# Streamed attention weights in row blocks of 128 x 1536 instead of column blocks of 640 x 384, with five ring slots instead of three

## The chip, the cores and the metric

The kernel runs on one core of one Trainium2 chip. The metric is the device time of that core in microseconds (us), the median over several executions. The kernel before was measured again beside every experiment. Its median lay between 2383 and 2409 us from one batch of runs to another, so kernels of different batches are compared by their ratio to the kernel before of the same batch.

## The reference, cut to what matters

```python
# x: 2048 x 640, H = 32 heads, Dh = 192, M = 8 memory tokens, seg = 32 tokens, all bf16
mem = mem0
for s in range(64):
    xs = x[:, s*32:(s+1)*32, :]
    h  = concatenate([mem, xs], axis=1)            # 40 rows x 640
    q, k, v = h@Wq, h@Wk, h@Wv                     # 640 x 6144 each
    p  = softmax(masked(q@k^T * Dh**-0.5))         # per head, 40 x 40
    o  = (p@v) @ Wo                                # 6144 x 640
    mem = o[:, :8, :]                              # the next segment needs it
    outs.append(o[:, 8:, :])
a = concatenate(outs)
b = gelu(x@w_gate) * (x@w_up) @ w_down             # 640 -> 1536 -> 640
g = sigmoid(sum(x * gate_w))
out = g*a + (1-g)*b
```

The 64 segments form a chain: the memory rows that one segment returns are inputs of the next. Each segment multiplies only 40 rows with all four attention matrices (31.5 MB). The memory plan of each kernel has room for only a part of them (47 of 64 pieces before, 61 of 84 after). That part stays resident, and the rest is loaded again in every segment.

## The kernel before

The attention weights are cut into 64 pieces of 480 KB. A Q, K or V piece is 128 partitions x (5 row blocks x 384 columns), that is, all 640 rows of two heads. A Wo piece is three row blocks of 128 x 640. 47 pieces are resident. 17 are streamed in every segment through a ring of three slots, by DMAs that the SP engine issues. A streamed piece is first copied once to a contiguous scratch in HBM and read from there.

```python
B_RING = int(opts.get("ring", 3))
...
def piece_src(m, t):
    if m == 0:
        return Wq2[:, :, 384 * t:384 * t + 384]        # [p, k, n]: 5 row blocks x 384 columns
    ...
    return Wo2[:, 3 * t:3 * t + 3, :]
...
def piece(seg, m, t):
    ...
    while done <= pos:
        slot = stream_counter[0] % B_RING
        if not (seg == 0 and done < B_RING):
            S_.add("sp", lambda e, slot=slot, done=done: e.dma_start(ring_flat[slot], wscr[done]),
                   reads=[Rg("dw", done, done + 1)], writes=[r_ring[slot]],
                   dma_sem="ring%d" % slot, name="ring s%d p%d" % (seg, done))
```

A load into a slot waits until the matmuls that read the slot's last piece are done. The Q and K projections take one piece at a time, chunk by chunk, with the row blocks innermost. The score matmuls of a group of four heads use eight tiles of 128 rows and then eight of 64 rows, because a head has 192 columns:

```python
def qk_pair(s, pr):
    for ti in range(2):
        for m in range(2):
            pv_, pr_ = piece(s, m, t)
            for cc in range(3):
                for k in range(KT):                    # KT = 5, innermost
                    fns.append(... e.matmul(ps[:, bank, slot*R:(slot+1)*R], pv_[:, k, cc*128:(cc+1)*128],
                                   Hb[hb][:, k, :], start=(k == 0), stop=(k == KT - 1)))   # L826
...
def scores(s, o):
    ...
    fa.append(... Q[:, qs, :], Q[:, ks, :], tile_position=(0, 0) ...)
    fa.append(... Q[:, qs + 2, :], Q[:, ks + 2, :], tile_position=(0, 64) ...)
    fb.append(... Q[0:64, qs + 1, :], Q[0:64, ks + 1, :], tile_position=(0, 0) ...)
    fb.append(... Q[64:128, qs + 1, :], Q[64:128, ks + 1, :], tile_position=(64, 64) ...)
    S_.add("pe", fa + fb, ...)
```

The order of work in a segment ends with `("wo", 3), ("pt", 3), ("wo", 4), ("pv", 3), ("wo", 5), ("wo", 6), ("wo", 7)`: "pt" transposes the probabilities of the last heads, "pv" multiplies them with V, and each "wo" is 30 matmuls of the output projection.

Of the kernel before, what the change touches and what calls it, by code (L numbers as in the profile page):

```python
# [221 lines left out]
def _build(nc, A_x, A_mem0, A_Wq, A_Wk, A_Wv, A_Wo, seg_len, w_gate, w_up, w_down,  # L222
# [23 lines left out]
    PIECE = KT * 384 * 2  # L246
    assert 3 * Dm * 2 == PIECE
# [21 lines left out]
    wsA["Hx"] = al(2 * KT * 128 * 2)  # L269
# [7 lines left out]
    wsA["xr4"] = al(Dm * 2)  # L277
    NQB, NVB, NPB, NUB = 3, 2, 2, 2
    wsB["QKT"] = al(NQB * 12 * R * 2)
    wsB["v"] = al(NVB * 768)  # L280
    wsB["vl"] = al(NOCT * 768)
    wsB["p"] = al(NPB * 4 * 64 * 2)
# [3 lines left out]
    wsB["stats"] = al(2 * 3 * 4 * 4)  # L286
    wsB["aT4"] = al(KT * 128 * 2)
    wsB["br4"] = al(Dm * 2)
# [15 lines left out]
    npieces = 4 * NT  # L304
    B_RING = int(opts.get("ring", 3))
    nslots = (total - wsA_total - wsB_total) // PIECE
    nres = min(npieces, nslots - B_RING)
    if "nres" in opts:
        nres = min(nres, int(opts["nres"]))
    nstream = npieces - nres  # L310
    if nstream == 0:
        B_RING = 0
    assert nres >= 0 and nres + B_RING <= nslots and (nstream == 0 or 2 <= B_RING <= nstream)
    arena_bytes = max((nres + B_RING) * PIECE + wsB_total, B_RING * PIECE + ffn_total) + wsA_total
    arena_bytes = al(arena_bytes)
    assert arena_bytes <= total, (arena_bytes, total)
# [6 lines left out]
    assert ffn_base >= B_RING * PIECE  # L323
    ring_off = [j * PIECE for j in range(B_RING)]
    res_off = [(B_RING + j) * PIECE for j in range(nres)]
    o = wsA_base - wsB_total
    assert o >= (nres + B_RING) * PIECE
# [15 lines left out]
    slot_class = []  # L343
    for j in range(nres):
        end = res_off[j] + PIECE
        if end <= ffn_base:
            slot_class.append(0)
        elif end <= ffn_off["wd"]:
            slot_class.append(1)
        else:  # L350
            slot_class.append(2)
    late_slots = [j for j in range(nres) if slot_class[j] > 0]

# [14 lines left out]
    Hx = [bview(o_Hx + b * KT * 256, KT * 256).rearrange("p (k t) -> p k t", t=128) for b in range(2)]  # L368
    r_Hx = [sreg(o_Hx + b * KT * 256, KT * 256) for b in range(2)]
# [15 lines left out]
    xr4 = bview(wsA_off["xr4"], Dm * 2)  # L385
    r_xr4 = sreg(wsA_off["xr4"], Dm * 2)
    QB = 12 * R * 2
    QKT = [bview(wsB_off["QKT"] + b * QB, QB).rearrange("p (s r) -> p s r", r=R) for b in range(NQB)]
    r_QKT = [sreg(wsB_off["QKT"] + b * QB, QB) for b in range(NQB)]
# [4 lines left out]
    pm_sb = [bview(wsB_off["p"] + b * 512, 256).rearrange("p (t k) -> p t k", k=L) for b in range(NPB)]  # L394
    pl_sb = [bview(wsB_off["p"] + b * 512 + 256, 256).rearrange("p (t k) -> p t k", k=L) for b in range(NPB)]
    r_p = [sreg(wsB_off["p"] + b * 512, 512) for b in range(NPB)]
# [13 lines left out]
    br4 = bview(wsB_off["br4"], Dm * 2)  # L410
    r_br4 = sreg(wsB_off["br4"], Dm * 2)
    r_br4h = [sreg(wsB_off["br4"], Dm * 2, 0, 4 * XA), sreg(wsB_off["br4"], Dm * 2, 4 * XA, 128)]
    r_xr4h = [sreg(wsA_off["xr4"], Dm * 2, 0, 4 * XA), sreg(wsA_off["xr4"], Dm * 2, 4 * XA, 128)]
    mem0r = br4
    r_mem0r = r_br4
    gwr = bview(wsB_off["aT4"], 256)
    r_gwr = sreg(wsB_off["aT4"], 256)
    assert wsB_off["aT4"] >= ffn_off["brow"] and wsB_off["br4"] >= ffn_off["brow"]
# [28 lines left out]
    def piece_src(m, t):  # L447
        if m == 0:
            return Wq2[:, :, 384 * t:384 * t + 384]
        if m == 1:  # L450
            return Wk2[:, :, 384 * t:384 * t + 384]
        if m == 2:
            return Wv2[:, :, 384 * t:384 * t + 384]
        return Wo2[:, 3 * t:3 * t + 3, :]

    def piece_view(m, o):
        if m == 3:
            return bview(o, PIECE).rearrange("p (c n) -> p c n", n=Dm)
        return bview(o, PIECE).rearrange("p (k n) -> p k n", n=384)

    PROG = [("qk", 0), ("qk", 1), ("qk", 2), ("sc", 0), ("v", 0), ("qk", 3), ("qk", 4), ("pt", 0), ("sc", 1),
            ("v", 1), ("qk", 5), ("pv", 0), ("qk", 6), ("pt", 1), ("sc", 2), ("v", 2), ("qk", 7), ("pv", 1),
            ("wo", 0), ("wo", 1), ("pt", 2), ("sc", 3), ("v", 3), ("pv", 2), ("wo", 2), ("wo", 3), ("pt", 3),
            ("wo", 4), ("pv", 3), ("wo", 5), ("wo", 6), ("wo", 7)]
    assert NOCT == 4
    COST = dict(qk=0.4, v=1.0, sc=0.45, pt=0.1, pv=0.45, wo=0.4)
# [3 lines left out]
    for kind, i in PROG:  # L470
        if kind == "qk":
            for ti in range(2):
                for m in range(2):
                    order.append((m, 2 * i + ti))
                    tcons.append(tt)
                    tt += COST[kind]
        elif kind == "v":
            for tl in range(4):
                order.append((2, 4 * i + tl))
                tcons.append(tt)  # L480
            tt += COST[kind]
        elif kind == "wo":
            for ti in range(2):
                order.append((3, 2 * i + ti))
                tcons.append(tt)
                tt += COST[kind]
        else:
            tt += COST[kind]
    tseg = tt + 0.6
    assert len(order) == npieces and len(set(order)) == npieces  # L490
    streamed = set()
    for k in range(nstream):
        target = (k + 0.5) * tseg / nstream
        best = min((i for i in range(npieces) if i not in streamed), key=lambda i: abs(tcons[i] - target))
        streamed.add(best)
    resident_list = [i for i in range(npieces) if i not in streamed]
    stream_list = [i for i in range(npieces) if i in streamed]
    res_slot = {}
    for k, i in enumerate(resident_list):
        res_slot[order[i]] = k  # L500
    stream_pos = {order[i]: k for k, i in enumerate(stream_list)}
    r_res = [sreg(o, PIECE) for o in res_off]
    r_ring = [sreg(o, PIECE) for o in ring_off]
    if nstream > 0:
        wscr = nc.dram_tensor("w_stream_scratch", (nstream, 128, PIECE // 2), BF, kind="Internal").ap()
    ring_flat = [bview(o, PIECE) for o in ring_off]
# [3 lines left out]
    order_index = {mt: i for i, mt in enumerate(order)}  # L510
    last_req = {}

    def piece(seg, m, t):
        oi = order_index[(m, t)]
        assert oi == last_req.get(seg, -1) + 1, "pieces must be consumed in `order`"
        last_req[seg] = oi
        if (m, t) in res_slot:
            j = res_slot[(m, t)]
            return piece_view(m, res_off[j]), r_res[j]
        pos = stream_pos[(m, t)]  # L520
        done = issued.get(seg, 0)
        while done <= pos:
            mm, tq = order[stream_list[done]]
            slot = stream_counter[0] % B_RING
            if not (seg == 0 and done < B_RING):
                S_.add("sp", lambda e, slot=slot, done=done: e.dma_start(ring_flat[slot], wscr[done]),
                       reads=[Rg("dw", done, done + 1)], writes=[r_ring[slot]],
                       dma_sem="ring%d" % slot, name="ring s%d p%d" % (seg, done))
            stream_counter[0] += 1
            ring_of[(seg, mm, tq)] = slot  # L530
            done += 1
        issued[seg] = done
        slot = ring_of[(seg, m, t)]
        return piece_view(m, ring_off[slot]), r_ring[slot]

    def resident_load_ops(classes):
        ops = []
        for k, i in enumerate(resident_list):
            if slot_class[k] not in classes:
                continue  # L540
            m, t = order[i]

            def reg(k=k, m=m, t=t):
                dst = piece_view(m, res_off[k])
                src = piece_src(m, t)
                S_.add("sp", lambda e: e.dma_start(dst, src), writes=[r_res[k]], dma_sem="res%d" % k,
                       name="res %d %d" % (m, t))
            ops.append(reg)
        return ops

    def relayout_ops():
        nb = B_RING
        seq = list(range(nb, nstream)) + [(nstream - nb + j) % nb for j in range(nb)]
        loads = []
        stores = []
        for i, k in enumerate(seq):
            slot = i % nb
            assert k >= nb or k == slot
            m, t = order[stream_list[k]]

            def ld(k=k, slot=slot, m=m, t=t):
                S_.add("sp", lambda e: e.dma_start(piece_view(m, ring_off[slot]), piece_src(m, t)),
                       writes=[r_ring[slot]], dma_sem="ring%d" % slot, name="relay ld %d" % k)

            def st(k=k, slot=slot):
# [526 lines left out]
```

## Time and profile before

| quantity | before | where it is read |
|---|---|---|
| median time | 2409.07 us (4 runs, 2389.05 to 2410.3) | the runs |
| span of the profiled execution | 2396.1 us | the page |
| PE busy | 86% | the page |
| time of one segment | 34.31 us | mean distance of the memory copies on ACT |
| start of segment 0's memory copy | 230.4 us | the same |
| PE waits for streamed weights, from 232 us on | 120 us | the waits view, summed over lines |
| PE waits named "issue", from 232 us on | 144 us | the same |
| PE waits for other engines, from 232 us on | 22 us | the same |

These are lines of the page of the kernel before: the busy times, two of the DMA queues (packets, MB, share of the 16 DMA engines), the shares of the chain of waits that ended last, the costliest group (busy us, mean ns, then the idle time before it and what ended most of it), and one line of the DMA issues (KB each, us from issue to landing).

```profile
span 2396.1 us, 128172 instructions
PE 2064.1 (86%) x60326; PEld 1704.8 (71%) x60326; DVE 852.3 (36%) x2880; ACT 629.3 (26%) x1432; POOL 37.9 (2%) x181
...
q1 hardware_dynamic: 201578, 581.72, 76.4%
...
q8 instruction: 471, 7.72, 1.3%
...
PE 55%; DMA 38%; issue 6%; SPq 0%; ACT 0%; DVE 0%; DVEq 0%
...
L826 PE MATMUL ps<-arena 128*128 128x40 bf16 x30720 | 902.9, 182 | 190.3 <-issue 104.4
...
arena<-w_stream_scratch SPq DMA_DIRECT2D x1085, 480.0 KB, 4.5
```

PE (matmuls) and PEld (weight loads, which overlap them: 2064.1 and 1704.8 us busy in a span of 2396.1) are the busiest engines, and everything else is far from full. The chain is PE 55% and DMA 38%: by this line alone, the streamed weights seem worth a third of the time. The waits view shows how much PE stands. These are its largest lines for PE (line, waited for; us in total, times, longest us):

```profile
PE ps L826 <- issue: 104.4, 122, 2.5
...
PE ps L826 <- DMA arena<-w_stream_scratch: 57.8, 86, 2.1
...
PE ps L962 <- DMA arena<-w_stream_scratch: 33.9, 66, 2.5
...
PE ps L843 <- DMA arena<-w_stream_scratch: 24.6, 45, 2.0
```

L826 is the Q and K projections, L962 is Wo and L843 is V. Two kinds of stop matter: a weight piece that has not landed, and "issue", where PE waits for nothing that the profile names. Both kinds show in the timeline of PE (start, duration, group; the wait just before it in brackets):

```profile
1008.43 0.53 PE L962 MATMUL ps<-arena 128*128 128x40 bf16 x15
1009.49 2.25 PE L962 MATMUL ps<-arena 128*128 128x40 bf16 x75 [0.52 <-DMA arena<-w_stream_scratch]
...
1015.70 1.07 PE L826 MATMUL ps<-arena 128*128 128x40 bf16 x32
1018.22 0.88 PE L826 MATMUL ps<-arena 128*128 128x40 bf16 x28 [1.45 <-issue]
```

The "issue" stop of 1.45 us falls in the middle of one run of L826 matmuls. Such stops are those of instruction fetch. The queue line has 471 instruction transfers with 7.72 MB, 16 KB each, and PE runs 120,652 instructions (60,326 matmuls and as many weight loads), that is 471 blocks of 256. Counting PE's instructions in blocks of 256, in the records of the trace from about 200 us on, 159 of the 343 gaps over 0.5 us between weight loads stand at one of two neighbouring places of the block in the kernel before (the others include the waits for weights).

### The profile page before, as it was taken

The numbers are of one execution on the slowest core, as the hardware profiler recorded it, in microseconds if no ns is written. First come the engines' busy times: TensorE is split into PE (matmuls) and PEld (weight loads), VectorE is DVE, ScalarE is ACT, GpSimd is POOL, SyncE is SP. The second block draws the span as 40 slices with busy tenths as digits, with TensorE's granted clock in tenths as the row PEclk, the third lists the DMA queues.
The fourth block names the chain that finished last, engine by engine and source line by source line (L and its number), as shares of the span: only waits on it lengthen the run. The fifth ranks groups of instructions, "written<-read, shape, count | busy, mean of one in ns | idle before, by whom it ended". The sixth has DMA issues, their size and how long they took to land.

```text
span 2396.1 us, 128172 instructions
## 1 busy us (share of the span) xinstructions
PE 2064.1 (86%) x60326; PEld 1704.8 (71%) x60326; DVE 852.3 (36%) x2880; ACT 629.3 (26%) x1432; POOL 37.9 (2%) x181
## 2 busy tenths in 40 slices
PE   7997888888889888898888888888888888888887
PEld 3455777777777777777777777777777777777776
DVE  2222343333334333343334333333433333333333
ACT  2222222222222222222222222222222222222222
POOL 0000000000000000000000000000000000000000
PEclk9998999999999999999999999999999999999999
DMA  8868878787887887777787878777887777878777
GB/s 291 275 199 262 255 251 250 248 263 246 254 252 252 256 254 250 258 244 245 250 262 239 254 249 252 251 246 249 248 265 234 239 253 249 260 244 257 244 241 231
DMA packets 210940, 600.41 MB, mean 251 GB/s; under 512 B 19426, under 2 KB 68074, under 8 KB 210410
## 3 DMA queue, kind: packets, MB, share of 16 engines
q1 hardware_dynamic: 201578, 581.72, 76.4%
q10 hardware_dynamic: 8832, 10.49, 1.3%
q8 instruction: 471, 7.72, 1.3%
q14 instruction: 59, 0.48, 0.1%
HBM read 578.53 MB, written 13.60 MB: 247 GB/s over the span
## 4 chain that ended last, share of the span: by engine, by line
PE 55%; DMA 38%; issue 6%; SPq 0%; ACT 0%; DVE 0%; DVEq 0%
DMA arena<-w_stream_scratch 37%; PE ps L826 24%; PE ps L843 11%; PE ps L962 7%; PE ps L726 2%; PE ps L723 2%; PE ps L741 2%; PE ps L933 1%; PE ps L881 1%; PE ps L865 1%; DMA arena<-in_B_w_up_dram 1%; PE ps L877 1%; PE ps L935 0%; PE ps L744 0%; ACT arena L1002 0%
## 5 line engine op out<-in xcount | busy, mean ns | idle before, releaser
L826 PE MATMUL ps<-arena 128*128 128x40 bf16 x30720 | 902.9, 182 | 190.3 <-issue 104.4
L826 PEld LDWEIGHTS ps<-arena 128*128 128x128 bf16 x30720 | 845.0, 97 | 292.9 <-issue 182.6
L830 ACT ACTIVATE arena<-ps 128x480 bf16<-128x480 f32 x512 | 291.9, 570 | 867.2 <-PE ps L826 859.3
L962 PE MATMUL ps<-arena 128*128 128x40 bf16 x15360 | 446.8, 180 | 42.8 <-DMA arena<-w_stream_scratch 33.9
L962 PEld LDWEIGHTS ps<-arena 128*128 128x128 bf16 x15360 | 422.4, 96 | 64.4 <-DMA arena<-w_stream_scratch 45.3
L843 PE MATMUL ps<-arena 128*32 128x384 bf16 x6400 | 338.4, 348 | 35.4 <-DMA arena<-w_stream_scratch 24.6
L916 DVE TENSOR_TENSOR arena<-ps,arena 128x320 bf16<-128x320 bf16 x256 | 125.8, 491 | 397.2 <-PE ps L914 397.2
L843 PEld LDWEIGHTS ps<-arena 128*32 128x32 bf16 x6400 | 154.1, 100 | 125.2 <-DMA arena<-w_stream_scratch 30.9
L893 DVE TENSOR_REDUCE arena<-ps 104x4 f32<-104x160 f32 x256 | 81.3, 318 | 319.6 <-PE ps L883 319.2
L947 DVE CAST arena<-ps 64x160 bf16<-64x160 f32 x256 | 80.6, 315 | 261.4 <-PE ps L935 261.3
L897 ACT ACTIVATE ps<-ps 104x160 f32<-104x160 f32 x256 | 71.9, 281 | 350.4 <-DVE ps L895 350.4
L943 ACT ACTIVATE arena<-ps 128x320 bf16<-128x320 f32 x256 | 111.2, 434 | 183.0 <-PE ps L935 183.0
L850 ACT ACTIVATE arena<-ps 128x384 bf16<-128x384 f32 x256 | 124.8, 488 | 43.8 <-PE ps L843 42.6
L933 PE MATMUL ps<-arena 128*128 128x160 bf16 (+1 forms) x768 | 131.4, 259 | 4.6 <-issue 2.1
L935 PE MATMUL ps<-arena 128*128 128x64 bf16 (+1 forms) x768 | 126.0, 203 | 2.9 <-issue 2.8
L899 DVE TENSOR_REDUCE arena<-ps 104x4 f32<-104x160 f32 x256 | 83.1, 325 | 99.7 <-ACT ps L897 98.2
L933 PEld LDWEIGHTS ps<-arena 128*128 128x128 bf16 x768 | 73.6, 98 | 33.4 <-issue 12.3
L895 DVE TENSOR_TENSOR ps<-ps,arena 104x160 f32<-104x160 f32 x256 | 85.1, 332 | 8.8
L949 DVE CAST arena<-ps 64x160 bf16<-64x160 f32 x256 | 83.9, 328 | 7.9
L881 PE MATMUL ps<-arena 64*40 64x40 bf16 x1024 | 71.0, 182 | 12.4 <-DMA arena<-w_stream_scratch 8.0
L1004 DVE CAST arena<-ps 128x120 bf16<-128x120 f32 x64 | 18.1, 282 | 168.1 <-ACT arena L1002 166.3
L903 DVE TENSOR_TENSOR arena<-ps,arena 104x128 bf16<-104x128 f32 x256 | 74.6, 291 | 8.8
(73 smaller groups left out, 1473.6 us busy)
## 6 DMA issues: line engine op xcount, KB each, us to landing
arena<-w_stream_scratch SPq DMA_DIRECT2D x1085, 480.0 KB, 4.5
w_stream_scratch<-arena SPq DMA_DIRECT2D x17, 480.0 KB, 6.9
arena<-in_A_Wv_dram SPq DMA_DIRECT2D x16, 480.0 KB, 7.3
arena<-in_A_Wk_dram SPq DMA_DIRECT2D x16, 480.0 KB, 7.0
arena<-in_A_Wq_dram SPq DMA_DIRECT2D x16, 480.0 KB, 5.7
arena<-in_A_Wo_dram SPq DMA_DIRECT2D x16, 480.0 KB, 8.9
arena<-in_A_x_dram SPq DMA_DIRECT2D x4, 640.0 KB, 7.1
ffn_b_scratch<-arena ACTq DMA_DIRECT2D x16, 160.0 KB, 5.5
```

The costliest lines, as they stand in the source:

```text
L826: e.matmul(ps[:, bank, slot * R:(slot + 1) * R], pv_[:, k, cc * 128:(cc + 1) * 128], Hb[hb][:, k, :], start=(k == 0), stop=(k == KT - 1)))
L830: S_.add("act", lambda e: e.activation(out=QKT[b], in_=ps[:, bank, 0:12 * R].rearrange("p (s r) -> p s r", r=R), func=ACTF.Copy), reads=[r ...
L843: fns.append(lambda e, k=k, j=j: e.matmul(ps[32 * j:32 * j + 32, bank, 0:384], lhs(k), pvs[j][0][:, k, :], start=(k == 0), stop=(k == KT - ...
L850: S_.add("act", lambda e: e.activation(out=v_sb[o % NVB], in_=ps[:, bank, 0:384], func=ACTF.Copy), reads=[r_ps[bank]], writes=[r_v[o % NVB ...
L881: fb.append(lambda e, Q=Q, o0=o0, qs=qs, ks=ks: e.matmul(o0, Q[0:64, qs + 1, :], Q[0:64, ks + 1, :], start=False, stop=True, tile_position ...
L895: S_.add("dve", lambda e: e.tensor_tensor(out=S3, in0=S3, in1=mxb, op=ALU.subtract), reads=[rb, rst], writes=[rb], name="smax sub")
L916: S_.add("dve", lambda e: e.tensor_tensor(out=PTm, in0=apx(pv[:, 512:616], [[64, 2], [0, 4], [1, R]]), in1=apx(mbd, [[0, 2], [1, 4], [0, R]]),
L933: return [lambda e: e.matmul(full, v[:, e0:e0 + 128], PTm[:, ia:ib], start=True, stop=False, skip_group_check=True), lambda e: e.matmul(pa ...
L935: lambda e: e.matmul(part, vl[:, e0:e0 + 128], PTl[:, ia:ib], start=False, stop=True, skip_group_check=True)]
L943: S_.add("act", lambda e: e.activation(out=apx(u[:, 0, 0, :], [[2 * R, 2], [3 * R, 4], [1, R]]), in_=ps[:, A, 0:2 * W].rearrange("p (c t r ...
L949: S_.add("dve", lambda e: e.tensor_copy(out=u[64:128, :, 1, :], in_=ps[64:128, B, W:2 * W].rearrange("p (t r) -> p t r", r=R)), reads=[r_p ...
L962: fns.append(lambda e, pv_=pv_, cc=cc, c=c, n=n, t=t, u=u: e.matmul(ps[:, OB, n * R:(n + 1) * R], pv_[:, cc, n * 128:(n + 1) * 128], u[:, ...
```

## The change

The intent is to make the ring deeper for little more memory (5 x 384 = 1920 KB instead of 3 x 480 = 1440 KB) and to do without the scratch copy. The Q, K and V weights are cut into row blocks: 128 rows x 1536 columns (eight heads) of 384 KB, read from the inputs as they lie. Wo pieces shrink from three row blocks to two (320 KB). 61 of 84 pieces are resident, 23 are streamed per segment (16 and 7), and the ring has five slots.

A row block feeds twelve column chunks, so the loops run the row blocks outermost, and twelve sums grow at once in one PSUM bank. Q and K have one buffer each instead of three shared ones. K is kept with zero rows, so that all sixteen score matmuls of a group use 128 rows. Some other buffers become single, which pays for memory.

```diff
-    PIECE = KT * 384 * 2
+    OW = 4 * 384
+    GQ = OW * 2
+    GO = 2 * Dm * 2
...
-    B_RING = int(opts.get("ring", 3))
+    B_RING = int(opts.get("ring", 5))
...
-            return Wq2[:, :, 384 * t:384 * t + 384]
+        return (Wq2, Wk2, Wv2)[m][:, k, OW * o_:OW * (o_ + 1)]
...
-        return Wo2[:, 3 * t:3 * t + 3, :]
+            return Wo2[:, 2 * key[1]:2 * key[1] + 2, :]
...
-            ("wo", 0), ("wo", 1), ("pt", 2), ("sc", 3), ("v", 3), ("pv", 2), ("wo", 2), ("wo", 3), ("pt", 3),
-            ("wo", 4), ("pv", 3), ("wo", 5), ("wo", 6), ("wo", 7)]
+            ("pt", 2), ("sc", 3), ("v", 3), ("pv", 2), ("wo", 1), ("wo", 2, 0), ("pt", 3), ("wo", 2, 1), ("pv", 3),
+            ("wo", 2, 2), ("wo", 3)]
...
-                S_.add("sp", lambda e, slot=slot, done=done: e.dma_start(ring_flat[slot], wscr[done]),
+            S_.add("sp", lambda e, slot=slot, key=key: e.dma_start(piece_view(key, ring_off[slot]), piece_src(key)),
...
-                for cc in range(3):
-                    for k in range(KT):
+        for k in range(KT):
+            g_, rg_ = piece(s, (m, o, k))
+            for i in range(12):
...
-            fb.append(... Q[0:64, qs + 1, :], Q[0:64, ks + 1, :], ... tile_position=(0, 0) ...)
-            fb.append(... Q[64:128, qs + 1, :], Q[64:128, ks + 1, :], ... tile_position=(64, 64) ...)
+            for ot, qi, ki, last in ((o0, 0, 2 * tl, False), (o1, 1, 12 + tl, False), (o0, 1, 8 + tl, True),
+                                     (o1, 2, 2 * tl + 1, True)):
+                fns.append(... e.matmul(ot, Qs[:, qi, :], Ks[:, ki, :], start=False, stop=last, ...))
```

(The score lines are shortened. Left out are the new buffer sizes, the split of the K evacuation into three ACT instructions, the V loop in the same row-block order, the removed scratch copies, and the moved loads of the x and b rows.)

The bytes streamed per segment hardly change: before 17 x 480 = 8160 KB, after 16 x 384 + 7 x 320 = 8384 KB.

## The prediction

> **What bounds it now.** The page: span 2396 us, PE busy 86%, DMA engines about 78%, ACT 26%, DVE 36%. The memory copies (ACT, L1002) run from 230.4 to 2357.7 us: 34.3 us per segment. The rest, about 235 us, is the feed-forward part and first segment, hardly touched. In the timeline, undisturbed matmuls come every 25 ns in projections and Wo, and 20 V matmuls take 0.82 us; summing a segment so (projections 12.0, V 4.1, Wo 6.0, scores, transposes and PV 4.6, boundary 0.5) gives about 27 us. Some 7 us per segment are stalls, of two kinds:
>
> 1. *Weight ring.* In groups and waits, PE stands for streamed weights in L826, L962, L843, L881: about 175 us, 2.8 us per segment. A load takes 4.5 us from issue to landing (DMA view). With three slots and 17 pieces per segment, by the sum above, 4.2 us on average (3.7 to 4.7) pass between a slot's release and the need of its next piece. That is under 4.5: the ring is latency-bound, not bandwidth-bound.
> 2. *Instruction fetch.* "issue" ended 104 us of L826's idle time on PE (182 us on weight loads). These gaps, up to 2.5 us, lie inside groups, 128 weight-load/matmul pairs apart, about 1.3 us after an instruction transfer ended. The queue line has 471 instruction transfers, 7.72 MB: 16 KB each. [...] A block of 256 seems to need some 4.2 us from entry to the next entry; 128 matmuls at 25 ns need 3.2. Half of all blocks stall, about 200 us in total.
>
> **What the change does.**
> - Ring: 23 pieces per segment (16 of 384 KB, 7 of 320 KB), five slots. Streamed bytes rise 2.7% (8.36 to 8.59 MB), packets from 2176 to 3840 per segment. Release to need becomes 5.5 us (least 5.0), so most ring waits should go: -2 to -2.5 us per segment. But a PE that no longer waits for weights meets the fetch limit earlier, so I count half: -70 us in all.
> - Scores: all sixteen matmuls use full rows, so one change of tile shape per group (0.11 against 0.02 us) goes: -0.3 us per segment, half kept, -10 us. [...] the trace shows these 0.1 us.
> - Last heads: 20 instead of 30 Wo matmuls stand between pT and PV, and between PV and the last Wo part, against a DVE latency near 1 us: +0.25 us twice per segment, half hidden, +15 us.
> - K evacuation becomes three ACT instructions (+0.5 us, 256 times); ACT stays near 32%. Single Q/K buffers are covered by 60 matmuls (1.5 us). No cost.
> - No relayout stores: the start is PE-bound, a few us at most.
> - Matmul count is unchanged.
>
> Sum: -65 to -70 us.
>
> **Predicted:** 2340 us, 2285 to 2400; faster 0.65, same 0.31, slower 0.04.
>
> **What would show it.** Ring waits on PE fall from 175 to under 60 us; "issue" idle of PE and its loads does not fall, probably grows; segment about 33.2 us; PE busy 88%; DMA share 78 to 84%; 471 to 475 instruction transfers.
>
> **What would make it wrong.** A busier DMA queue delaying instruction transfers (then the gain vanishes); small packets lengthening landing beyond 5.5 us; or fetch stalls shrinking too (then 2290 or less).

-70 us for the ring, -10 for the scores and +15 for the last heads are -65. The halvings are estimates.

## More of the kernel before

PE resumes about 1.4 us (1.23 to 1.58) after an instruction transfer ends.

## The result, and the profile after

The changed kernel takes 2284.6 us (median of four runs, 2281.36 to 2294.34) against 2409.07 us. The ratio is 0.9509, with a 95% interval of 0.9451 to 0.9567. A ratio here is the mean time of one kernel's runs over that of the other's runs of the same rounds, so it is not quite the ratio of the medians.

These are the page lines of the changed kernel that answer to those of before:

```profile
span 2285.0 us, 129546 instructions
PE 1990.3 (87%) x60326; PEld 1653.2 (72%) x60326; DVE 839.4 (37%) x2880; ACT 726.0 (32%) x1944; POOL 38.2 (2%) x182
...
q1 hardware_dynamic: 285274, 580.96, 80.2%
...
q8 instruction: 471, 7.72, 1.4%
...
PE 72%; issue 10%; DVE 4%; DMA 3%; ACT 1%; SPq 0%; DVEq 0%
...
L761 PE MATMUL ps<-arena 128*128 128x40 bf16 x30720 | 855.6, 180 | 135.2 <-issue 110.8
...
arena<-in_A_Wk_dram SPq DMA_DIRECT2D x398, 384.0 KB, 4.3
arena<-in_A_Wo_dram SPq DMA_DIRECT2D x465, 320.0 KB, 4.2
```

The DMA share of the chain falls from 38% to 3%. Yet the span falls by only 111 us, under 5%: a share of the chain is no amount that can be gained. The waits view of the changed kernel shows what took the place of the ring waits (L761 is Q and K, L818 the scores, L786 V, L869 PV, L898 Wo):

```profile
PE ps L761 <- issue: 110.8, 159, 2.4
...
PE ps L818 <- issue: 41.1, 39, 2.3
PE ps L786 <- issue: 35.4, 41, 1.9
...
PE ps L869 <- DVE arena L855: 18.1, 64, 0.3
PE ps L898 <- DVE arena L885: 15.2, 54, 0.7
```

No line of streamed weights is left among the large ones; "issue" has spread to the scores and to V. The last two lines are new: the last heads now wait for the DVE between transposes, PV and Wo. Both kinds are in the timeline:

```profile
1007.51 0.24 PE L869 MATMUL ps<-arena 128*128 128x160 bf16 x1 [0.28 <-DVE arena L855]
...
1017.49 3.02 PE L761 MATMUL ps<-arena 128*128 128x40 bf16 x114
1021.86 0.32 PE L761 MATMUL ps<-arena 128*128 128x40 bf16 x6 [1.35 <-issue]
```

Undisturbed matmuls follow each other by about 25 ns in both kernels (3.02 us for 114 here, from which the 0.18 us of the last one is to be taken off). The windows view compares the segments as a whole, from 232 us to the end, first before and then after (the window; its length; busy us of PE, PEld, DVE, ACT and POOL with counts; granted clock; DMA share; GB/s):

```profile
232.00:2391.90 2159.90, 1862.85 (x58338) 1593.03 (x58333) 792.38 (x2753) 573.57 (x1337) 33.22 (x154) 0.96 0.79 250
```

```profile
232.00:2281.00 2049.00, 1783.43 (x58056) 1535.32 (x58056) 778.29 (x2747) 664.85 (x1831) 32.80 (x152) 0.99 0.86 270
```

PE's busy time is 79 us shorter for nearly the same count of matmuls (the same 232 us are a slightly different point of the program), and the granted clock has gone from 0.96 to 0.99. Where the 111 us between the two profiled spans went, from 232 us on:

| part | before, us | after, us | difference, us |
|---|---|---|---|
| PE waits for streamed weights | 120 | 4 | -116 |
| PE waits named "issue" | 144 | 200 | +56 |
| PE waits for other engines | 22 | 53 | +31 |
| half-clock time of PE (difference: estimate below) | 178 | 64 | about -28 |
| start of segment 0's memory copy | 230.4 | 221.3 | -9 |
| PE's own time at the score matmuls (start to next start, waits left out) | 111 | 81 | -30 |
| rest, not accounted for | | | about -15 |

For the clock row I summed the stretches in which the granted clock was half. In such a stretch a matmul follows the last by 33 ns instead of 25, so an estimate of the gain is (178 - 64) x (1 - 25/33) = 28 us. By the first two rows, about half of what the ring waits lost came back as "issue". A segment takes 32.68 us on average instead of 34.31; over 63 segments that is 103 us, and with the 9 us of the start it is the whole difference.

### The profile page after: what moved, and what is told of

Same layout as the page of the kernel before. It is cut to its first block, busy times and chain, and to the rows that moved or that the text cites. A ratio compares the mean times of both kernels' runs of the same rounds, so it can differ in the third digit from the quotient of the medians.

```text
span 2285.0 us, 129546 instructions
## 1 busy us (share of the span) xinstructions
PE 1990.3 (87%) x60326; PEld 1653.2 (72%) x60326; DVE 839.4 (37%) x2880; ACT 726.0 (32%) x1944; POOL 38.2 (2%) x182
## 3 DMA queue, kind: packets, MB, share of 16 engines
q1 hardware_dynamic: 285274, 580.96, 80.2%
## 4 chain that ended last, share of the span: by engine, by line
PE 72%; issue 10%; DVE 4%; DMA 3%; ACT 1%; SPq 0%; DVEq 0%
PE ps L761 34%; PE ps L898 14%; PE ps L786 12%; PE ps L869 4%; PE ps L818 2%; DMA arena<-in_A_Wo_dram 2%; PE ps L807 2%; DVE arena L852 1%; PE ps L871 1%; DVE arena L885 1%; ACT arena L797 1%; DMA arena<-in_A_Wv_dram 1%; DVE arena L883 1%; DVE arena L855 1%; ACT arena L939 1%
## 5 line engine op out<-in xcount | busy, mean ns | idle before, releaser
L761 PE MATMUL ps<-arena 128*128 128x40 bf16 x30720 | 855.6, 180 | 135.2 <-issue 110.8
L761 PEld LDWEIGHTS ps<-arena 128*128 128x128 bf16 x30720 | 814.9, 96 | 186.8 <-issue 150.4
L898 PE MATMUL ps<-arena 128*128 128x40 bf16 x15360 | 441.7, 180 | 27.6 <-DVE arena L885 15.2
L898 PEld LDWEIGHTS ps<-arena 128*128 128x128 bf16 x15360 | 420.2, 96 | 42.5 <-DVE arena L885 21.4
L786 PE MATMUL ps<-arena 128*32 128x384 bf16 x6400 | 328.3, 335 | 36.9 <-issue 35.4
L768 ACT ACTIVATE arena<-ps 64x160 bf16<-64x160 f32 (+1 forms) x768 | 234.7, 340 | 351.6 <-PE ps L761 345.4
L749 ACT ACTIVATE arena<-ps 128x480 bf16<-128x480 f32 x256 | 146.0, 570 | 446.0 <-PE ps L818 324.0
L786 PEld LDWEIGHTS ps<-arena 128*32 128x32 bf16 x6400 | 150.5, 97 | 122.9 <-issue 53.3
L869 PE MATMUL ps<-arena 128*128 128x160 bf16 (+1 forms) x768 | 139.1, 262 | 26.7 <-DVE arena L855 18.1
L869 PEld LDWEIGHTS ps<-arena 128*128 128x128 bf16 x768 | 72.6, 98 | 102.4 <-DVE arena L830 34.3
L818 PE MATMUL ps<-arena 128*40 128x40 bf16 x4096 | 100.5, 181 | 41.2 <-issue 41.1
L818 PEld LDWEIGHTS ps<-arena 128*40 128x40 bf16 x4096 | 86.2, 98 | 45.6 <-issue 45.6
```

Source lines behind the costliest of these rows:

```text
L749: S_.add("act", lambda e: e.activation(out=Qs, in_=ps[:, 0, 0:12 * R].rearrange("p (s r) -> p s r", r=R), func=ACTF.Copy), reads=[r_ps[0]] ...
L761: fns.append(lambda e, i=i, sl=sl, k=k, g_=g_: e.matmul(ps[:, m, sl * R:(sl + 1) * R], g_[:, i * 128:(i + 1) * 128], Hb[hb][:, k, :], star ...
L768: S_.add("act", lambda e: e.activation(out=dst, in_=ps[plo:phi, 1, lo * R:hi * R].rearrange("p (s r) -> p s r", r=R), func=ACTF.Copy), rea ...
L786: return [lambda e, j=j: e.matmul(ps[32 * j:32 * j + 32, bk, 0:384], lhs, g_[:, 384 * j:384 * (j + 1)], start=(k == 0), stop=(k == KT - 1) ...
L818: fns.append(lambda e, ot=ot, qi=3 * tl + qi, ki=ki, last=last: e.matmul(ot, Qs[:, qi, :], Ks[:, ki, :], start=False, stop=last, skip_grou ...
L869: return [lambda e: e.matmul(full, v[:, e0:e0 + 128], PTm[:, ia:ib], start=True, stop=False, skip_group_check=True), lambda e: e.matmul(pa ...
```

## The experiments

Two questions remain after the comparison. Were the ring waits the cause at all, and if so, why did a removal of 116 us of ring waits come with 56 us more of "issue"? And is instruction fetch, if that is what "issue" is, tied to the stream of weights? The theories at the start: (A) the deeper ring does nearly all of it, and part of its gain goes back to instruction fetch; (B) the form of the loops and pieces does it (longer runs of matmuls, smaller loads, score tiles), whatever the ring. The later expectations name the theories that they test. Theory D is judged at the end of this section.

Three numbers are used for all of them. Waits are PE's, from 232 us on, summed over the lines of the waits view. "Block" is the mean time between two successive entries into a block of 256 PE instructions where both entries were stalled (by 0.2 to 0.3 us or more). It takes only blocks in which fetch was late, 18 pairs of some 450 in a_half and 37 in a_ring3, against 191 in the changed kernel; it is not the mean pace of fetch. The times come in steps: 3.74, 4.02, 4.29, 4.57, 4.84 us and so on in the traces of the kernel before and of the changed one, about 0.274 us apart. "Load" is the mean size of a streamed load.

| kernel | ratio to before | ring waits | issue waits | block, us | load, KB | KB per segment |
|---|---|---|---|---|---|---|
| before | 1 | 120 | 144 | 4.88 | 480 | 8160 |
| b_ring4 | 0.9945 | 20 | 246 | 4.86 | 480 | 8640 |
| after | 0.9509 | 4 | 200 | 4.59 | 365 | 8384 |
| a_again | 0.9559 | 4 | 196 | 4.57 | 365 | 8384 |
| a_ring3 | 0.9887 | 185 | 45 | 4.57 | 368 | 7360 |
| a_ring4 | 0.9417 | 8 | 168 | 4.56 | 366 | 7680 |
| a_ring8 | 0.9921 | 0 | 266 | 4.82 | 364 | 9472 |
| a_cap3 | 0.9953 | 214 | 51 | 4.44 | 365 | 8384 |
| a_split | 1.0763 | 222 | 105 | 5.36 | 182 | 8384 |
| a_half (wrong result) | 0.8586 | 0 | 29 | 4.18 | 182 | 4192 |
| a_still (wrong result) | 0.8445 | 0 | 1 | 3.74 (one case) | none | 0 |

### b_ring4: the kernel before, with four slots

```diff
-    B_RING = int(opts.get("ring", 3))
+    B_RING = int(opts.get("ring", 4))
```

> The kernel before with four slots instead of three, nothing else (18 of 64 pieces streamed instead of 17). Theory A (the gain is the longer time between the release of a slot and the need of its next piece): that time becomes about 5.4 us, over the 4.5 us to landing, so PE's waits for streamed weights fall from about 175 to under 50 us, instruction-fetch stalls grow from about 200 to 260 us, and the time is 2300 to 2330 us. Theory B (the gain is the row tiling, the loop order, or reading the inputs as they lie): 2390 us or more.

Measured: 2372.51 us (2357.7 to 2379.3) against 2383.43, ratio 0.9945 (0.9904 to 0.9987). The run decides more than any other. Its waits view:

```profile
PE ps L826 <- issue: 136.5, 152, 2.8
...
PE ps L843 <- issue: 32.0, 36, 1.5
PE ps L962 <- issue: 29.4, 39, 1.8
...
PE ps L826 <- DMA arena<-w_stream_scratch: 23.6, 27, 4.4
```

The fourth slot took away 100 us of ring waits, as theory A wanted, and "issue" grew by 102 us. The sum, 264 before, is 266. In the old form, ring waits and fetch stops stand in for each other, and the ring alone is worth about half a per cent. Theory A as I had put it falls; the time that theory B named, 2390 us or more, was missed too. The fetch did not stay as it was, though: with 8640 KB instead of 8160 streamed per segment and more of it in flight, the next transfer starts later after an entry (see a_still).

### a_ring3: the changed kernel, with three slots

```diff
-    B_RING = int(opts.get("ring", 5))
+    B_RING = int(opts.get("ring", 3))
```

> The changed kernel with three slots instead of five (384 KB each, about 21 pieces streamed). Theory A: release to need falls to about 3.5 us, under the 4.3 us to landing, so a segment is bound by the ring at about 21 / 3 x 5.0 = 35 us; 2420 us or more, slower than the kernel before. Theory B: the tiling and loop order keep their gain, under 2330 us.

Measured: 2354.22 us (2343.7 to 2361.2), ratio 0.9887 (0.9855 to 0.9918). Both expectations missed. The ring waits came back:

```profile
PE ps L761 <- DMA arena<-in_A_Wq_dram: 100.8, 117, 8.7
...
PE ps L761 <- DMA arena<-in_A_Wk_dram: 41.5, 57, 2.1
...
PE ps L761 <- issue: 22.4, 39, 2.4
```

So the new form needs more than three slots: more than three of the five points of the gain are lost without the other two. Even so it beats the old form at three slots, because ring and issue waits together are 230 us instead of 264. The new form is worth something that is not the depth of the ring. One part of it may be that smaller slots leave room for more resident pieces: 7360 KB are streamed per segment instead of 8160.

### a_ring8: the changed kernel, with eight slots

```diff
-    B_RING = int(opts.get("ring", 5))
+    B_RING = int(opts.get("ring", 8))
```

> The changed kernel with eight slots. Theory A: ring waits are already nearly gone at five slots, so more slots give nothing; the room that they take from resident weights streams a few per cent more, so 2275 to 2310 us. Rival (depth itself keeps paying, because more loads in flight raise the rate): under 2250 us.

Measured: 2366.0 us (2354 to 2373), ratio 0.9921 (0.9883 to 0.9959). Both expectations missed. It was expected near the changed kernel, and it is slower than that by three and a half points or more (0.9559 and 0.9509 in the other batches). Three more slots leave room for fewer resident pieces, so 9472 KB are streamed per segment; on average 3.6 loads are in flight instead of 3.06. No ring wait is left, but fetch has taken over:

```profile
PE ps L761 <- issue: 133.2, 156, 2.9
```

### a_still: the changed kernel with no streaming after the first segment (wrong result)

```diff
-            S_.add("sp", lambda e, slot=slot, key=key: e.dma_start(piece_view(key, ring_off[slot]), piece_src(key)),
+            if seg == 0:
+              S_.add("sp", lambda e, slot=slot, key=key: e.dma_start(piece_view(key, ring_off[slot]), piece_src(key)),
```

> Wrong results on purpose: the ring is filled in the first segment only, and later segments use what lies in the slots; no weight traffic after that. It asks what sets the instruction-fetch stalls that are left (about 270 us). If the instruction transfers queue behind streamed weights, they come sooner without them, the block stalls nearly vanish, and the time is 2000 to 2090 us. If a block of 256 instructions takes 4.2 us whatever the queues hold, the time stays at 2220 us or more.

Measured: 2012.81 us, ratio 0.8445, as expected. From 232 us on:

```profile
232.00:2000.00 1768.00, 1707.22 (x57810) 1500.08 (x57807) 767.86 (x2730) 660.50 (x1826) 33.01 (x152) 1.00 0.03 9
```

PE is busy 1707 of 1768 us, at full clock, and "issue" comes to 1 us. The instructions of PE are the same and are fetched just as often (471 instruction transfers again), so the fetch stops of 200 us need the weight stream beside them. That is shown: the fetch of instructions is slow because of the traffic of weights, not by itself. In the trace, the transfer of the next block starts 0.57 us (median) after PE entered a block here, 1.87 us after it in the changed kernel, 2.08 us in b_ring4. In the kernel before it is 1.87 us too. The transfer itself takes about 1 us in all of them.

### a_again: the changed kernel once more

> The changed kernel itself once more, as the anchor for the other three of this call: ratio to the kernel before 0.945 to 0.957 if the first comparison holds on this chip too.

Measured: 2280.04 us (2274.4 to 2287.2), ratio 0.9559 (0.9521 to 0.9598). It gives the second batch its own mark for comparison, and shows that two batches differ by half a point in this ratio.

### a_split: every load as two DMAs of 64 partitions

```diff
-            S_.add("sp", ... e.dma_start(piece_view(key, ring_off[slot]), piece_src(key)),
-                   writes=[r_ring[slot]], dma_sem="ring%d" % slot, ...)
+            for h in range(2):
+                S_.add("sp", ... e.dma_start(piece_view(key, ring_off[slot])[64*h:64*h+64], piece_src(key)[64*h:64*h+64]),
+                       writes=[r_ringh[slot][h]], dma_sem="ring%d_%d" % (slot, h), ...)
```

> The changed kernel with every streamed piece loaded by two DMAs of 64 partitions, same bytes, same slots. Theory C1: an instruction transfer waits behind the descriptors of one whole weight DMA on its DMA engine, so halving these brings instructions sooner: block-boundary stalls fall from about 270 to 200 us or less and the time by 1.5 to 3%. Theory C2: what counts is how many bytes of weights are queued, in whatever portions: within 1% of the changed kernel.

Measured: 2567.01 us, ratio 1.0763 (1.0718 to 1.0808). It was meant to halve the load size at the same number of bytes, and went the other way than expected. Its page:

```profile
q1 hardware_dynamic: 308826, 581.05, 89.9%
...
arena<-in_A_Wk_dram SPq DMA_DIRECT2D x768, 192.0 KB, 5.6
```

The same 3072-byte packets took 198 ns (median) instead of 121 when they went to 64 partitions, half a load took 5.6 us to land, and ring waits came back (222 us). Fetch became slower with the halved loads, not faster: the block is 5.36 us instead of 4.57, and an instruction transfer takes 1.26 us instead of 0.96. The run cannot tell what the size of a load does by itself, because it made all transfers slower at the same time. Two transfers to half the partitions each brought no gain here: the ratio is 1.0763 against 0.9559 of the unchanged kernel in the same batch. What theory C1 says of waiting behind one whole load was supposition, and this run does not show it.

### a_pt3: the last transposes one step earlier

```diff
-            ... ("wo", 1), ("wo", 2, 0), ("pt", 3), ("wo", 2, 1), ("pv", 3),
+            ... ("wo", 1), ("pt", 3), ("wo", 2, 0), ("wo", 2, 1), ("pv", 3),
```

> The changed kernel with the last probability transpose moved in front of the first third of the third Wo part, so that 40 matmuls instead of 20 stand between it and the PV matmuls that need its evacuation. The gap from Wo to PV is 465 ns in every segment now, against 25 ns undisturbed: 0.44 us x 64 = 28 us of waiting on DVE. If waits in front of PE simply add, 28 us or 1.2% less. If instruction fetch takes back about half, as with the ring waits, 10 to 18 us (0.5 to 0.8%).

Measured: 2302.56 us (2292.6 to 2309.6), ratio 0.9649 (0.9605 to 0.9693), against 0.9559 of the unchanged one in the same batch: slower by about 1%. The waits for other engines fell as intended, from 54 to 34 us. But issue waits rose by 39 us:

```profile
PE ps L761 <- issue: 152.0, 188, 3.4
```

A saved wait was more than paid back. The half-clock time grew too, from 50 us in a_again to 121, by the estimate above 17 us. Why saving a wait set this off stays open; a shift of the segment's work against the edges of the 256-instruction blocks would be one reason, and no run tests it.

### a_oldsc: the old order of the score matmuls in the changed kernel

```diff
-            for ot, qi, ki, last in ((o0, 0, 2 * tl, False), (o1, 1, 12 + tl, False), (o0, 1, 8 + tl, True),
-                                     (o1, 2, 2 * tl + 1, True)):
+            for ot, qi, ki, cp in ((o0, 0, 2 * tl, 0), (o1, 2, 2 * tl + 1, 64)):
+                fns.append(... Qs[:, qi, :], Ks[:, ki, :], ... tile_position=(0, cp) ...)
+            for ot, qi, ki, lo in ((o0, 1, 8 + tl, 0), (o1, 1, 12 + tl, 64)):
+                fb.append(... Qs[lo:lo + 64, qi, :], Ks[lo:lo + 64, ki, :], ... tile_position=(lo, lo) ...)
```

> The changed kernel with the score matmuls in the old array tiling (eight of 128 rows, then eight of 64 rows on the split chunk). This costs one more tile-shape change per group of scores, 0.11 against 0.02 us, 256 times: 22 us if it all adds, 8 to 15 us (0.4 to 0.7%) if instruction fetch hides part. Rival: the score tiling is where most of the gain over the four-slot version of the old kernel (about 85 us) comes from: 60 us or more.

Measured: 2286.33 us (2278.1 to 2290.8), ratio 0.958 (0.954 to 0.962), against 2280.04 us and 0.9559: no difference that the intervals allow. Its issue waits are 168 us instead of 196; these are the largest lines of it (first) and of a_again (second):

```profile
PE ps L761 <- issue: 89.5, 131, 2.6
...
PE ps L761 <- issue: 106.2, 153, 2.5
```

PE's own time at the scores, waits left out, is 106 us here and 81 in a_again. The 25 us more are nearly what the issue waits lost: PE spends them at the scores instead of waiting for instructions. The zero rows in K saved work, but the saved time came back as fetch waits.

### a_half: every load after the first segment brings half its bytes (wrong result)

```diff
-            S_.add("sp", ... e.dma_start(piece_view(key, ring_off[slot]), piece_src(key)),
+            S_.add("sp", ... if seg == 0 else ... e.dma_start(
+                piece_view(key, ring_off[slot])[:, 0:OW // 2] if key[0] < 3 else piece_view(key, ring_off[slot])[:, 0:1],
+                piece_src(key)[:, 0:OW // 2] if key[0] < 3 else piece_src(key)[:, 0:1]),
```

> Wrong results on purpose: from the second segment on, each streamed load brings only half of its piece (the same number of loads, slots and waits, half the bytes). Theory D: an instruction transfer is late by the bytes of weights that are in flight ahead of it (0 KB: a block takes 3.05 us from entry until its successor is there; about 875 KB with three slots: 3.86; about 1110 KB: 4.30). With some 500 KB in flight I expect 3.5 to 3.7 us, block stalls under 100 us, and 2040 to 2110 us. Rival: the number of loads, or any weight traffic at all, sets the delay: 4.1 us or more, and over 2200 us.

Measured: 2059.8 us, ratio 0.8586, inside the expectation. Its waits view:

```profile
PE ps L763 <- issue: 15.7, 39, 2.2
...
PE ps L788 <- issue: 8.8, 22, 0.9
```

With as many loads and slots as before, half the bytes take away 171 of the 200 us of fetch stops, and the next block's transfer starts 1.18 us after PE enters a block instead of 1.87. This is a dose between a_still and the changed kernel, and it answers in between. It changes the size of a load, of its packets and the total at once, so it does not say which of them counts. (The "block" of 4.18 us is above the 3.5 to 3.7 expected, but it comes from the 18 late pairs alone. The parts, 1.18 us to the start, about 1 us of transfer and 1.4 us until PE resumes, make 3.6.)

### a_cap3: at most three loads in flight

```diff
-                   writes=[r_ring[slot]], dma_sem="ring%d" % slot, name="ring s%d p%d" % (seg, done))
+                   writes=[r_ring[slot], Rg("tok", stream_counter[0] % 3, stream_counter[0] % 3 + 1)], dma_sem="ring%d" % slot, ...)
```

> The changed kernel in which a load is issued only when the third load before it has landed, so at most three are in flight (now 3.1 on average, four or five about half of the time). Theory D: fewer bytes in flight, so instructions come sooner, and three in flight still bring a piece every 1.3 to 1.4 us: ratio to the kernel before 0.935 to 0.952. If the ring waits come back as much as the fetch stalls shrink, 0.952 to 0.965.

Measured: 2385.63 us (2379 to 2394), ratio 0.9953 (0.9909 to 0.9997). The expectation missed. Three loads in flight at 4.4 us each allow 23 loads in 23 / 3 x 4.4 = 33.7 us, and a segment took 34.17 us: the cap itself became the limit. Ring waits are 214 us, the largest line being

```profile
PE ps L786 <- DMA arena<-in_A_Wv_dram: 74.1, 80, 2.3
```

A limit of three is thus too low in this form: the landing time of 4.2 to 4.4 us has to be covered by more than three loads (four slots are enough, see a_ring4). Fetch itself was quicker: a transfer starts 1.45 us after an entry instead of 1.88, and the issue waits are 51 us. What that would be worth without the ring waits, this run cannot say. The expectation also had the changed kernel wrong: it has four or five loads in flight for 22% of the time, not about half.

### a_ring4: the changed kernel, with four slots

```diff
-    B_RING = int(opts.get("ring", 5))
+    B_RING = int(opts.get("ring", 4))
```

> The changed kernel with four slots (22 pieces streamed, about 3% fewer bytes). Theory D: fetch stalls fall below the 270 us of five slots, to about 180, and ring waits rise to about 110 us; the two nearly cancel, ratio 0.950 to 0.968. With the lead-time theory alone (no fetch coupling) it would be slower by all of the ring waits, ratio 0.985 or more.

Measured: 2258.23 us (2257.3 to 2263.3), ratio 0.9417 (0.9388 to 0.9446). It is better than the expected range of 0.950 to 0.968, because the ring waits did not come back. It is the fastest correct kernel, about 1% under the changed kernel's time in the same batch (a_relay below, 2280.36). Four slots leave two more pieces resident, so 7680 KB are streamed instead of 8384. The ring waits rise only from 4 to 8 us (about 110 were expected), the issue waits fall from 200 to 168, and the largest issue line has become smaller:

```profile
PE ps L761 <- issue: 87.4, 140, 2.2
```

### a_relay: the scratch copy brought back in the changed kernel

```diff
+    wscr = nc.dram_tensor("w_stream_scratch", (nstream, 128, OW), BF, kind="Internal").ap()
...
+            if seg == 0 and done < B_RING:
...                                                     (the load as it was)
+            else:
+                S_.add("sp", ... e.dma_start(bview(ring_off[slot], piece_size(key)), wscr[done][:, 0:piece_size(key) // 2]),
+                    reads=[Rg("dw", done, done + 1)], writes=[r_ring[slot]], ...)
...                                                     (and one copy of each streamed piece at the start)
```

> The changed kernel with the relayout put back: the streamed pieces are copied once, at the start, into a contiguous scratch in HBM, and all loads after the first five come from there. If the layout that the loads read does not matter (a row of a piece is 3 KB or 1.25 KB contiguous either way at the input, 3 KB or 2.5 KB at the scratch), the ratio stays at 0.950 to 0.962. If reading the inputs as they lie is a part of the gain, 0.97 or more; if contiguous pieces are cheaper, under 0.945.

Measured: 2280.36 us (2275 to 2294), ratio 0.9514 (0.9473 to 0.9555), the same as the changed kernel. Where the streamed weights lie makes no difference to the whole time: the copies let segment 0 end 11 us later (its memory copy starts at 232.2 instead of 221.3 us), and the segments are a little shorter in turn (32.43 us instead of 32.57 to 32.68).

### What the experiments say together

Shown: PE's fetch of instructions is held up by the weight stream (issue waits of 1 us in a_still and 29 in a_half, against 200). Shown: in the old form, taking ring waits away with a fourth slot gives nearly all of it back as fetch waits (b_ring4: 100 us of ring waits less, 102 of "issue" more). Shown: the new form without the deeper ring gains about 1% and with it about 5% (a_ring3, a_again), and the source layout and the score order have no part in it (a_relay, a_oldsc).

Theory D, that a transfer is late by the bytes of weights in flight, can be tested in the traces themselves. For every entry into a block from 232 us on, I counted the weight loads that had been issued and had not landed, and took the time until the next instruction transfer started:

| kernel | KB in flight at an entry, mean | transfer starts after an entry, median us |
|---|---|---|
| a_still | 0 | 0.6 |
| a_half | 446 | 1.17 |
| a_ring3 | 880 | 1.51 |
| a_ring4 | 1043 | 1.82 |
| a_cap3 | 1083 | 1.45 |
| before | 1119 | 1.87 |
| after | 1169 | 1.88 |
| b_ring4 | 1239 | 2.07 |
| a_ring8 | 1323 | 2.01 |

But for a_cap3 the order is nearly that of the bytes. Inside one kernel it is the same: 1.57, 1.83 and 2.20 us on average with two, three and four loads in flight in the changed kernel, 1.70 and 2.35 with two and three in the kernel before. At some 1400 to 1450 KB the old form has 2.34 to 2.35 us (three loads) and the new 2.14 to 2.24 (four), so the size of a load, or something that goes with it, is left with 0.1 to 0.2 us. This is a relation in the traces; no run changed the bytes in flight alone. It also shows what the new form did not do: over all entries, transfers start as late after the change as before. They start sooner than in b_ring4, the old form with the ring waits gone.

What makes a block shorter in the new form, 4.59 instead of 4.88 us among late blocks, is only argued. The size of a load fits: with loads of 364 to 368 KB the block is 4.56 to 4.59 us for 7360, 7680 and 8384 KB per segment, so over that range the total does not matter, and 0, 182, 365 and 480 KB give 3.74, 4.18, 4.59 and 4.88 us. The packets changed with the load, from 3840 bytes at 149 ns (median) to 3072 bytes at 121 ns. How a larger load or packet would lengthen a block was not shown. Against size alone stand a_split with 5.36 us at 182 KB and a_ring8 with 4.82 us at 364 KB. The size of packets and the new order of instructions have not been separated from it either.

## Why the prediction was right or wrong

The direction, the class (faster) and most of the mechanism were right. The size was too small: 2340 us against 2284.6, at the very low end of the range (2285).

- *Ring waits on PE fall from 175 to under 60 us.* Right. On the matmul row they went from 120 us (the 175 included the waits of weight loads) to 4. The landing time was 4.2 to 4.4 us; the 5.5 us from release to need, on which the step rests, were not measured.
- *"Issue" does not fall, probably grows.* Right: 144 to 200 us.
- *Landing might lengthen with small packets.* It did not: 4.5 us before, 4.2 to 4.4 after, although there are 285,274 packets instead of 201,578.
- *PE busy 88%, DMA share 78 to 84%, 471 to 475 instruction transfers, segment 33.2 us.* Measured: 87%, 83% (the four queue lines of the page summed), 471, and 32.68 us.
- *Scores save 10 us.* Gross the order is worth 25 to 30 us, net nothing (a_oldsc). The prediction halved the saving for fetch, but fetch took all of it.
- *Last heads cost 15 us.* The waits came, 31 us more for other engines. But removing 20 us of them made the kernel 1% slower (a_pt3), so they are not a cost that can be subtracted.
- *K evacuation +0.5 us, ACT near 32%.* Measured: one instruction of 437 ns and two of 292 ns instead of one of 570 ns, so 0.45 us, and ACT 32%.
- *No relayout: a few us at most.* Segment 0 ended 9 us earlier. But a_relay with the copies, which starts 11 us later, was as fast overall.

What was mis-sized is the sum, "-65 to -70 us": the medians differ by 124 us, and the profiled spans, which the table of differences takes apart, by 111. It is not the halving in it, "so I count half: -70 us in all". In that table 116 us of ring waits went and 56 us of "issue" came, 60 us net, so the share came out near a half. That is in part luck, because there is no fixed share. b_ring4 lost 100 us of ring waits and got 102 us of issue waits: there the transfers also start 0.2 us later than before (median), which for its 280 stalled blocks of 455 is an estimate of 56 us, about half of what came back. a_ring4 lost 112 us of ring waits and got only 24 back.

What the sum lacked, by the same table: the clock, about 28 us, for which it had no term; PE's own time at the scores, 30 us where it had 10; and the earlier end of segment 0, 9 us where it had "a few us at most". Against that stand 31 us of waits for other engines where it had 15, and about 15 us are not accounted for. These parts cannot be credited one at a time: a_oldsc shows that the score time alone buys nothing, since fetch takes it. The prediction had tied a time of 2290 or less to "fetch stalls shrinking too". The time came, and the stalls grew.

Not foreseen at all was the clock. The records of the granted clock have stretches at half, nearly all 3.413 us long (47 of 51 before, 18 of 20 after); from 232 us on their sum went from 178 to 64 us, some 28 us of time by the estimate above. The traces do not show what brings one on: in the 3.4 us before such a window PE was never idle throughout, but waited for 1.1 to 2.3 us in all and ran at least 32 matmuls, before and after alike. The sum of waits alone does not tell it: with 266 us of ring and issue waits b_ring4 had a mean granted clock of 0.964, and with 265 us a_cap3 had 0.974.

A last point concerns the reading of "issue" as fetch. The trace has 471 transfers of 16 KB for 120,652 instructions, one for every 256, and their crossings are not hidden: 67% of the block entries of the changed kernel are stalled, 49% of those of the kernel before. Without the weight stream PE stands 1 us in all for them (a_still).

## What to carry to other kernels

When the waits view of PE shows "issue" stops beside a busy DMA stream (here 144 us before and 200 after, at a DMA share of 0.79 and 0.86), look whether they stand at a fixed distance (here 256 instructions, 227 of 249 long gaps at one place of the block) before you count the gain of anything else. Work or waits saved between two such stops came back as a longer stop here: about half (after) or nearly all (b_ring4, a_oldsc), but 24 of 112 us in a_ring4. What went with quicker fetch in this case was fewer bytes of weights in flight: the next transfer started 0.6 us after an entry at 0 KB, 1.17 at 446, 1.88 at 1169. Four slots, which leave two more pieces resident than five (ratio 0.9417), beat both five (0.9509) and eight (0.9921); their loads landed in 3.9 to 4.1, 4.2 to 4.4 and 4.6 to 4.7 us. Test the one-line change to the old kernel first (here its ring depth, 0.9945), since it tells whether the wait that the profile names is the one that pays.
